# The up product of three more pairs by a scheme of 15 block products, its sums of weights and inputs kept in the gate stage's tiles

## Chip, core and metric

One Trainium2 chip, of which the kernel uses one core. The metric is the device time of one execution in microseconds, as the median of three runs. Inputs and outputs are in fp32.

## What is computed

A gated recurrence (attention) is followed by a low-rank mixer and a two-layer MLP.

```python
# attention, B=4, H=8, S=768, D=48; a is scaled to magnitude <= 0.999 first
for t in range(S):
    S_re, S_im = a_re[t]*S_re - a_im[t]*S_im + outer(k[t], v[t]), a_re[t]*S_im + a_im[t]*S_re
    y[t] = q[t] @ S_re
x = y.transpose(0, 2, 1, 3).reshape(B, S, 384)
# mixer: U is 768x32, V is 32x768, w_ch1 is 384x1536, w_ch2 is 1536x384
u = x + (x.transpose(0, 2, 1) @ U @ V).transpose(0, 2, 1)
out = u + np.maximum(u @ w_ch1, 0) @ w_ch2
```

The change is in `u @ w_ch1`, here called the up product.

## The kernel before

The 4 x 768 tokens are cut into 24 chunks of 128 (`NCH` = 6 chunks to a batch). Most chunks are worked in groups of two. For a group, `gates` (L529) makes the decay factors from a_re and a_im in the tiles x, y, n, z, ar and ai, each of which has one buffer. `prep` (L662) weights and rotates q and k on DVE, transposes them on PE and evicts them with ACT into one of three QK buffers, the ring of L393. `chain` (L691) forms the products within a chunk (`inner`, `corners`), scales QK between them on DVE (`times`, recorded as L329), and carries the state from chunk to chunk (`dk`, `y`).

When the six chunks of a batch are done, three pairs of chunks go through `mixer` (L857), so m runs from 0 to 11: batch 0 gives pairs 0 to 2, batch 3 gives pairs 9 to 11. For each pair the low-rank term is added, u is transposed into uT (L907), the up product fills h, and the down product (`down_two`, L1064, from pair 1 on) adds into the output tile xo. The pairs of one batch run beside the attention of the next batch; only pairs 9 to 11 run alone, at the end.

There are two forms of the up product.

- Plain (`up`, L910), for pairs 0 to 8: 36 matmuls of 128x128 weights with 256 token columns. A group of six fills a PSUM bank, and one ACT Relu of 128x512 evicts it into h.
- `up_fewer` (L922), for pairs from FEWER = 9 on (L227). w_ch1 is seen as 3x3 blocks `a(i, j)` (i is a third of the 1536 outputs, which is four times 128; j is a 128-row block of inputs), and uT as 3x2 blocks `b(j, k)` (k is the chunk of the pair). The plain product is 18 block products. The scheme makes 15 from sums of weight blocks (`combine`, L1006: 13 DVE instructions of 128x512, once) and sums of inputs (L939: 10 DVE instructions for each pair). Each block product is four matmuls of 128x128 with 128 columns, so 60 to a pair. They run in five PSUM accumulations A to E that are not cleared between steps: after every step the running sum is taken out, either copied into a part of h by ACT (L975, six times) or added to it by DVE (L977, recorded as L332, nine times). The next step of the same accumulation has to wait for that. When a part is complete, ACT applies Relu to it (six times). Before the change A and B lie in the PSUM banks tagged Y and C to E in those tagged A, which attention also uses. The combined weights c(0) to c(7) and the input sums x(0) to x(11) lie in the three QK buffers, which are free by then.

The order of all instructions is made in advance by `Plan` (L45): each step is recorded with an engine, a cost, a rank and the buffers it needs; a list scheduler then picks for each engine the ready step of the lowest rank. The ranks of attention steps come from the table URGENCY, and `urgency` (L253) gives the products of the MLP the rank n + 1000 and the small steps around it n - 1000. The engines run exactly this order. While PE has nothing planned before the first MLP product, it issues filler matmuls on the identity (L1222).

Of the kernel before, what the change touches and what calls it, by code (L numbers as in the profile page):

```python
# [23 lines left out]
BLK = 32  # L24

URGENCY = {
    "w1": {0: -424.24, 1: 801.16, 2: -941.63, 3: 764.55, 4: 813.86, 5: -255.72, 6: 1013.64},
    "w2": {0: -182.39, 2: -4.99, 4: 984.13, 6: -117.56, 8: -114.39, 10: -7.53, 12: -119.07},
    "gates": {0: -53.85, 1: -240.4, 2: -197.04, 4: -1081.73, 6: -28.82, 8: -131.88, 10: -81.91, 12: 806.19, 14: -135.86,
        16: -172.78, 18: -1235.03, 20: -1238.39, 22: -793.35},  # L30
    "angles": {0: -716.01, 1: -1088.81, 2: -1448.91, 4: -1014.2, 6: -162.99, 8: 28.61, 10: -297.82, 12: 644.75,
        14: 834.98, 16: 897.12, 18: 629.83, 20: 664.93, 22: -754.36},
    "prep": {0: -721.6, 1: -435.35, 2: -1258.46, 3: -186.16, 4: -178.84, 5: -818.35, 6: -144.43, 7: 728.1, 8: -1457.09,
        9: -198.24, 10: 551, 11: 946.21, 12: -172.65, 13: -5.89, 14: -408.17, 15: -519.54, 16: -1135.98,
        17: -956.56, 18: -1131.69, 19: -157.67, 20: -96.66, 21: 899.53, 22: 814.34, 23: -381.52},
    "levels": {0: 564.72, 1: -778.93, 2: -86.7, 3: -537.84, 4: -1278.59, 5: -136.91, 6: 701.9, 7: 776.18, 8: -1127,
        9: -702.85, 10: -795.56, 11: 2.07, 12: -1232.03, 13: -1063.51, 14: -1125.58, 15: 974.76, 16: 79.03,
        17: -1073.03, 18: 681.53, 19: -464.62, 20: 687.22, 21: -956.1, 22: -13.2, 23: -550.79},
    "rest": {0: -161.27, 1: -1281.74, 2: -47.49, 3: -331.17, 4: -871.19, 5: -748.68, 6: -223.21, 7: -779.64,
        8: -191.99, 9: -545.57, 10: -436.36, 11: -535.13, 12: -1262.49, 13: -76.97, 14: -253.25, 15: -455.92,  # L40
        16: -157.31, 17: -92.4, 18: -977.97, 19: 625.7, 20: -1238.92, 21: -243.55, 22: -90.76, 23: 790.73},
}


# [144 lines left out]
def kernel(  # L189
# [34 lines left out]
    DH = DM // 2  # L224

    PLAIN = 1
    FEWER = B * (S // CH) // 2 - 3  # L227
    NCH = S // CH
    NT = B * NCH
    HH = H // 2  # L230
# [70 lines left out]
    def PE(*a, **kw):  # L301
        plan.add("PE", *a, late=0.17, **kw)
# [87 lines left out]
    AT, DG, VP = [], [], []  # L390
    QKC = singles.tile([128, H, 2, DP], FP, name="QKC")
    nc.gpsimd.memset(QKC, 0.0)
    QKS = [singles.tile([128, 2, H, CH], FP, name="QK%d" % n) for n in range(3)]  # L393
    TS = []
    for n in range(3):
        TS.append(singles.tile([DQ, GC, H * NTOT], FP, name="T%d" % n))
# [45 lines left out]
    def load_a(g):  # L442
        lo, hi = GROUPS[g]
        for nm, src in (("ar", a_re), ("ai", a_im)):
            buffer((nm, g), nm, 1, [128, GC, H, D])
            for i in range(lo, hi):
                SP(c_dma(DM), ("load", (0, 0.5, 3)[g] if g < 3 else lo + 3), lambda nm=nm, src=src, i=i: nc.sync.dma_start(
                    out=get(nm, g)[:, i - lo], in_=rows(src, i)), writes=[(nm, g, i)])
# [80 lines left out]
    def gates(g):  # L529
# [13 lines left out]
            return get(*b)[:, (i - lo) * DM:(i - lo + 1) * DM]  # L543

        def magnitudes():
            for b in (x, y, n):
                buffer(b, "g" + b[0], 1, [128, GC * DM])
            ring(l, "GL", GL)
            ACT(ca, R1, lambda: act(t(x), t(ar), AF.Square), [ar], [x])
            ACT(ca, R1, lambda: act(t(y), t(ai), AF.Square), [ai], [y])  # L550
            DVE(cd, R1, lambda: add(t(x), t(x), t(y)), [y], [x])
            DVE(c_one(W), R1, lambda: nc.vector.tensor_scalar(out=t(x), in0=t(x), scalar1=M2LO, scalar2=M2HI, op0=OP.max,
                                                              op1=OP.min), [], [x])
            ACT(ca, R1, lambda: act(t(n), t(ar), AF.Abs), [ar], [n])
            table(ca, R1, lambda: act(t(l), t(x), AF.Ln), [x], [l])
            table(ca, R1, lambda: act(t(x), t(l), AF.Exp, scale=0.5), [l], [x])
            DVE(cd, R1, lambda: add(t(x), t(x), t(n)), [n], [x])
            table(ca, R1, lambda: act(t(y), t(l), AF.Exp, scale=-0.5, bias=leps), [l], [y])
            table(ca, R1, lambda: act(t(y), t(y), AF.Ln, bias=1.0), [], [y])

            ACT(ca, R1, lambda: act(t(l), t(l), AF.Relu, scale=-0.5, bias=lmax), [], [l])
            DVE(cd, R1, lambda: nc.vector.scalar_tensor_tensor(out=t(l), in0=t(l), scalar=LNMAX, in1=t(y), op0=OP.subtract,
                                                               op1=OP.add), [y], [l])
            table(ca, R1, lambda: act(t(x), t(x), AF.Ln), [], [x])
            table(ca, R1, lambda: act(t(x), t(x), AF.Exp, scale=-1.0), [], [x])
            DVE(cd, R1, lambda: mul(t(x), t(x), t(ai)), [ai], [x])
            ACT(ca, R1, lambda: act(t(n), t(ar), AF.Sign, bias=tiny), [ar], [n])
            for i in range(lo, hi):
                within(i)
# [36 lines left out]
                  [e + (i,)])  # L606

        def turns():
            buffer(z, "gz", 1, [128, GC * DM])

            table(ca, R2, lambda: act(t(x), t(x), AF.Arctan), [], [x])
            DVE(cd, R2, lambda: nc.vector.scalar_tensor_tensor(out=t(z), in0=t(x), scalar=math.pi / 4, in1=t(n),
                                                               op0=OP.subtract, op1=OP.mult), [x, n], [z])
            ACT(ca, R2, lambda: act(t(z), t(z), AF.Identity, scale=1.0 / math.pi, bias=fourth), [], [z])
            for i in range(lo, hi):
                angles(i)
# [45 lines left out]
    def prep(i):  # L662
        R1 = "prep", i
        g = group_of(i)
        qk, QK = ("qk", i), ("QK", i)
        ring(QK, "QK", [a[0:DQ] for a in QKS])
        def weigh():
            a = get(*qk).rearrange("p u h d -> p u (h d)")
            mul(a, a, get("es", i))
# [187 lines left out]
    def mixer(m):  # L857
# [52 lines left out]
        def up(ff):  # L910
# [8 lines left out]
            PE(2.6, RM, products, [uT] + [("w1", f, lo) for f in range(KD)], [ps], takes=[h], steps=4 * KD)  # L919
            ACT(c_act(2 * N), R0, lambda: act(get(*h)[:, ff:ff + 2], get(*ps), AF.Relu), [ps], [h + (ff,)])  # L920

        def up_fewer():  # L922

            if m == FEWER:
                for n in range(3):
                    ring(("wc", n), "QK", [a.rearrange("p u h t -> p (u h t)") for a in QKS])
                combine()
            n3, B0, RU = KF // 3, ("bc", m), ("small", m)  # L930

            def b(j, k):
                return get(*uT)[:, j, k * CH:(k + 1) * CH]

            def x(n, w=1):
                return get("wc", 2)[:, n * CH:(n + w) * CH]

            def put(w, o, a, b, op, reads=(), writes=()):
                DVE(c_dve(w * CH), RU, lambda: nc.vector.tensor_tensor(out=o(), in0=a(), in1=b(), op=op), [uT] + list(reads),  # L939
                    [("wc", 2, n) for n in writes])  # L940

            flat = lambda lo, hi: get(*uT).rearrange("p f t -> p (f t)")[:, lo * CH:hi * CH]
            many = lambda a, w: a.unsqueeze(1).to_broadcast([128, w, CH])
            put(3, lambda: x(0, 3).rearrange("p (w t) -> p w t", t=CH), lambda: flat(0, 3).rearrange("p (w t) -> p w t", t=CH),
                lambda: many(b(1, 1), 3), OP.subtract, (), (0, 1, 2))
            put(1, lambda: x(3), lambda: b(0, 0), lambda: b(1, 0), OP.subtract, (), (3,))
            put(1, lambda: x(4), lambda: x(3), lambda: b(2, 0), OP.add, [("wc", 2, 3)], (4,))
            put(1, lambda: x(5), lambda: x(4), lambda: b(1, 1), OP.add, [("wc", 2, 4)], (5,))
            put(1, lambda: x(6), lambda: b(2, 1), lambda: x(4), OP.subtract, [("wc", 2, 4)], (6,))
            put(2, lambda: x(7, 2).rearrange("p (w t) -> p w t", t=CH), lambda: flat(0, 2).rearrange("p (w t) -> p w t", t=CH),  # L950
                lambda: many(b(2, 1), 2), OP.add, (), (7, 8))
            put(1, lambda: x(9), lambda: b(0, 1), lambda: b(0, 0), OP.subtract, (), (9,))
            put(1, lambda: x(10), lambda: b(0, 0), lambda: b(2, 0), OP.add, (), (10,))
# [6 lines left out]
            def chain(tag, steps):  # L960

                ps = ("few", (m, tag))
                psum(ps, "Y" if tag in "AB" else "A", [128, n3, CH])
                for n, (w, v, to) in enumerate(steps):
                    def products(n=n, w=w, v=v):
                        for q in range(n3):
                            nc.tensor.matmul(out=get(*ps)[:, q], lhsT=w()[:, q * 128:(q + 1) * 128], rhs=v[0](), start=(n == 0 and q == 0),  # L967
                                             stop=True, skip_group_check=True)
                    PE(0.9, RM, products, [uT, ("w1", 0, 0)] + [("wc", 0), ("wc", 1)] + [("wc", 2, k) for k in v[1]], [ps], takes=[h],
                       steps=2 * n3)  # L970
                    i, k = to
                    o = ("part", (m, i, k))
# [12 lines left out]
                return lambda: w1[:, j, i * n3 * 128:(i + 1) * n3 * 128]  # L985

            def c(n):
                return lambda: get("wc", n // 4)[:, n % 4 * n3 * 128:(n % 4 + 1) * n3 * 128]

            def u(j, k):  # L990
                return (lambda: b(j, k)), ()
# [14 lines left out]
        def combine():  # L1006
# [6 lines left out]
            def a(i, j):  # L1013
                return w1[:, j, i * n3:(i + 1) * n3]

            def c(n):
                return get("wc", n // 4)[:, n % 4 * n3:(n % 4 + 1) * n3]

            def put(n, x, y, op, reads=()):
                DVE(c_dve(n3), RC, lambda: nc.vector.tensor_tensor(out=c(n), in0=x(), in1=y(), op=op),  # L1020
                    [("wc", k // 4, k % 4) for k in reads], [("wc", n // 4, n % 4)])
            sub_, add_ = OP.subtract, OP.add
            put(6, lambda: a(2, 0), lambda: a(2, 1), add_)
            put(4, lambda: c(6), lambda: a(0, 1), sub_, (6,))
# [158 lines left out]
                        mixer(m)  # L1183


    waits, later, done = [], [], 0
    for g in range(NG):
        load_a(g)
# [89 lines left out]
```

## Time and profile before

| | us |
|---|---|
| median of three runs | 710.96 (710.59 to 711.04) |
| the profiled execution | 709.66 |
| its span in the trace | 707.9 |
| PE busy | 687.1 (97%) |
| DVE busy | 517.9 (73%) |
| ACT busy | 406.6 (57%) |
| granted PE clock, mean over the span | 0.992 |

Busy times are sums over one engine's instructions; what a change is worth in a stage depends on which engine ends last there. In the trace an fp32 product on PE appears as two records: 324 plain matmuls of the nine plain pairs are the 648 records of L917. The ends of PE records are modelled, so a stall of PE is read from the starts of its instructions and not from gaps in its busy time.

### The profile page before, as it was taken

What the parts mean: (1) busy time and instruction counts of PE and PEld (TensorE: products, weight loads), DVE (VectorE), ACT (ScalarE), POOL (GpSimd) and SP (SyncE); (2) the same over time, 40 slices, a digit from 0 to 9 for tenths busy, and PEclk for the clock granted to TensorE, in tenths of its full rate; (3) what the DMA queues carried; (4) which work ended last, traced back from release to release, by engine and by line L of the source; (5) the groups of instructions that cost most, each with busy time, mean ns of one, the idle gap of its engine ahead of it and who ended that gap; (6) DMA issues with size and microseconds to landing.
All of it is one profiled execution on the core that took longest, in us unless ns stands there. A gap on an engine that the chain in (4) does not pass through costs nothing.

```text
span 707.9 us, 26672 instructions
## 1 busy us (share of the span) xinstructions
PE 687.1 (97%) x12004; PEld 599.7 (85%) x12004; DVE 517.9 (73%) x823; ACT 406.6 (57%) x760; POOL 51.3 (7%) x92
## 2 busy tenths in 40 slices
PE   7989998999999999999999999999999999999998
PEld 6877877877688898888898888888898897999997
DVE  5899998887899787858788578375693665555734
ACT  6796987677797796969695945532413223041230
POOL 5110000011010000001001011000000000000000
PEclk9999998899999999999999999999999999999999
DMA  7876855489423433324134041221201010000000
GB/s 186 180 183 146 179 103 145 92 197 179 103 59 69 87 66 87 72 67 102 20 76 97 5 97 26 52 53 37 48 16 37 3 40 1 12 13 23 6 19 22
DMA packets 165265, 53.22 MB, mean 75 GB/s; under 512 B 154080, under 2 KB 160416, under 8 KB 165152
## 3 DMA queue, kind: packets, MB, share of 16 engines
q1 hardware_dynamic: 161072, 42.26, 27.5%
q0 software_dynamic: 4080, 9.27, 5.6%
q8 instruction: 94, 1.54, 0.9%
q14 instruction: 19, 0.16, 0.1%
HBM read 33.59 MB, written 4.72 MB: 54 GB/s over the span
## 4 chain that ended last, share of the span: by engine, by line
PE 76%; ACT 10%; DVE 7%; issue 3%; DMA 2%; SPq 1%; DVEq 0%; ACTq 0%
PE down L1099 20%; PE up L917 17%; PE few L967 6%; PE inner L717 5%; PE tr L683 5%; PE dk L803 3%; PE y L842 3%; PE down L1056 2%; PE ks ps L788 2%; PE es ps L575 2%; DVE QK L329 2%; ACT x L326 2%; PE y L834 2%; PE ph L633 2%; PE spare L1222 1%
## 5 line engine op out<-in xcount | busy, mean ns | idle before, releaser
L329 DVE TENSOR_TENSOR QK<-QK,T 112x1024 f32<-112x1024 f32 x120 | 145.1, 1217 | 8.1 <-PE corners L767 7.1
L917 PE MATMUL up<-uT,w 128*128 128x256 f32 x648 | 150.2, 383 | 0.0
L917 PEld LDWEIGHTS up<-uT,w 128*128 128x128 f32 x648 | 119.9, 190 | 17.7 <-issue 0.6
L326 ACT ACTIVATE h<-up 128x512 f32<-128x512 f32 x54 | 32.0, 593 | 75.1 <-PE up L917 66.4
L1099 PE MATMUL down<-w,h 128*128 128x192 f32 x396 | 73.5, 330 | 0.0
L686 ACT COPY QK<-tr 112x512 f32<-112x512 f32 x96 | 52.4, 586 | 33.0 <-PE tr L683 32.6
L1099 PEld LDWEIGHTS down<-w,h 128*128 128x128 f32 x396 | 64.0, 190 | 2.9 <-issue 1.3
L1222 PE MATMUL spare<-ident 128*128 128x128 f32 x438 | 62.2, 292 | 1.8 <-POOL ident masks.py:199 1.4
L1222 PEld LDWEIGHTS spare<-ident 128*128 128x128 f32 x438 | 56.0, 201 | 5.7 <-issue 2.0
L717 PEld LDWEIGHTS inner<-QK 112*32 112x32 f32 x4608 | 45.4, 110 | 13.8 <-issue 8.7
L683 PE MATMUL tr<-ident,QKC 128*112 128x128 f32 x384 | 52.8, 275 | 1.5 <-DVE QKC L329 0.9
L717 PE MATMUL inner<-QK 112*32 112x16 f32 (+1 forms) x4608 | 50.7, 190 | 3.3 <-issue 2.9
L329 DVE TENSOR_TENSOR QKC<-qk,cs 128x768 f32<-128x768 f32 x48 | 45.7, 952 | 11.0 <-PE tr L683 6.6
L332 DVE TENSOR_TENSOR xo<-down,xo 128x192 f32<-128x192 f32 (+1 forms) x79 | 29.5, 384 | 29.4 <-PE down L1099 27.5
L683 PEld LDWEIGHTS tr<-ident,QKC 128*112 128x112 f32 x384 | 42.3, 133 | 9.6 <-ACT QK L686 2.5
L1043 POOL DMA_DIRECT2D out_dram<-xo x32 | 18.5, 577 | 332.5 <-DVE xo L332 307.8
L772 ACT COPY AT<-corners 32x128 f32<-32x128 f32 x96 | 24.5, 255 | 31.3 <-PE corners L767 30.3
L975 ACT COPY h<-few 128x512 f32<-128x512 f32 x18 | 10.4, 582 | 51.6 <-PE few L967 51.6
L851 ACT COPY xo<-y 64x192 f32<-64x192 f32 x96 | 30.0, 312 | 11.5 <-PE y L842 10.3
L1099 PE MATMUL down<-stage 128*128 128x192 f32 x198 | 36.6, 328 | 0.0
L723 DVE COPY_PREDICATED DG<-mask,inner 128x128 f32<-128x128 int32 (+1 forms) x72 | 24.3, 340 | 15.7 <-PE inner L717 12.6
L332 DVE TENSOR_TENSOR h<-few,h 128x512 f32<-128x512 f32 x27 | 18.7, 691 | 23.0 <-PE few L967 22.2
(131 smaller groups left out, 1227.3 us busy)
## 6 DMA issues: line engine op xcount, KB each, us to landing
stage<-in_moe_w_ch_dram SPq DMA_DIRECT2D x12, 768.0 KB, 7.5
ar<-in_a_re_dram SPq DMA_DIRECT2D x24, 192.0 KB, 3.4
ai<-in_a_im_dram SPq DMA_DIRECT2D x24, 192.0 KB, 3.7
qk<-in_q_dram SPq DMA_DIRECT2D x24, 192.0 KB, 3.1
qk<-in_k_dram SPq DMA_DIRECT2D x24, 192.0 KB, 4.0
VP<-in_v_dram SPq DMA_DIRECT2D x24, 192.0 KB, 3.8
w<-stage POOLq DMA_DIRECT2D x12, 384.0 KB, 6.0
T<-E SPq DMA_DIRECT2D x44, 96.0 KB, 2.4
```

The source lines that it names most:

```text
L326: return nc.scalar.activation(out=o, in_=i, func=f, **kw)
L329: nc.vector.tensor_tensor(out=o, in0=a, in1=b, op=OP.mult)
L332: nc.vector.tensor_tensor(out=o, in0=a, in1=b, op=OP.add)
L683: nc.tensor.transpose(out=get(*ps)[0:DQ, j], in_=get(*qkc)[:, hh * HH + j].rearrange("p u d -> p (u d)")[:, 0:DQ], identity=ident)
L686: ACT(c_act(HH * CH) - 0.05, R1, lambda u=u, hh=hh, ps=ps: nc.scalar.copy(out=get(*QK)[:, u, hh * HH:(hh + 1) * HH], in_=get(*ps)[0:DQ]), ...
L717: nc.tensor.matmul(out=get(*ps)[js, h], lhsT=k_of(h)[:, js], rhs=part(q_of(h)[:, js], "p"), start=True, stop=True, tile_position=(0, j * BLK))
L772: ACT(0.32, RR, lambda r=r, u=u: nc.scalar.copy(out=get(*ATi).rearrange("p (a u) t -> p a u t", u=2)[r:r + BLK, :, u, BLK:2 * BLK], in_=ge ...
L851: ACT(c_act(HH * D), RR, lambda r=r, u=u: nc.scalar.copy(out=get(*xi).rearrange("p (a u d) -> p a u d", u=2, d=D)[r * HC:(r + 1) * HC, :, ...
L917: nc.tensor.matmul(out=get(*ps)[:, e], lhsT=w1[:, f, (ff + e) * 128:(ff + e + 1) * 128], rhs=get(*uT)[:, f], start=(f == 0), stop=(f == KD ...
L967: nc.tensor.matmul(out=get(*ps)[:, q], lhsT=w()[:, q * 128:(q + 1) * 128], rhs=v[0](), start=(n == 0 and q == 0), stop=True, skip_group_ch ...
L1099: nc.tensor.matmul(out=get(*to)[:, part], lhsT=x(j), rhs=y[:, j], start=(first and j == 0), stop=(j == KH - 1), skip_group_check=not first)
L1222: nc.tensor.matmul(out=spare[0], lhsT=ident, rhs=ident, start=True, stop=True)
```

## The change

The constant FEWER goes from 9 to 6, so pairs 6, 7 and 8 use the scheme as well; pairs 9 to 11 use it before and after. These three pairs run beside the attention of batch 3, which still needs the QK buffers, so the sums move. The six gate tiles become one tile GATE of six areas of 768 columns. When the last gate group is done, the first 512 columns of area n hold c(n) for n up to 5, the other 256 hold x(n) and x(n + 6), and a new tile holds c(6) and c(7). In the ring of each area the scheme's sums come after all the gate groups, so `combine` can only be ordered behind the last of them. QK becomes an ordinary pool of three. For pairs before the last batch the accumulations A and B lie in the PSUM banks tagged M, which up and down products share, and C, D and E in those tagged T, which the transposes share. The URGENCY table is another one throughout, so the order of the attention's instructions changes, by single places before the first MLP product and more widely after it.

```diff
-    "w1": {0: -424.24, 1: 801.16, 2: -941.63, ...
+    "w1": {0: 577.09, 1: -1319.32, 2: 484.43, ...
...
-    FEWER = B * (S // CH) // 2 - 3
+    FEWER = B * (S // CH) // 2 - 6
...
-    QKS = [singles.tile([128, 2, H, CH], FP, name="QK%d" % n) for n in range(3)]
+    GATE = singles.tile([128, 6, GC * DM], FP, name="gate")
+    AREA = {nm: GATE[:, n] for n, nm in enumerate(("x", "y", "n", "z", "ar", "ai"))}
+    AREA.update({nm: AREA[nm].rearrange("p (c h d) -> p c h d", h=H, d=D) for nm in ("ar", "ai")})
+    sums_w = singles.tile([128, 2, KF // 3 * 128], FP, name="sums")
...
-        ring(QK, "QK", [a[0:DQ] for a in QKS])
+        buffer(QK, "QK", 3, [DQ, 2, H, CH])
...
+        def mix_of(n):
+            return GATE[:, n, 0:KF // 3 * 128] if n < 6 else sums_w[:, n - 6]
+
+        def c_of(n):
+            return ("few", n, "w") if n < 6 else ("few", 0, "w%d" % n)
...
-            n3, B0, RU = KF // 3, ("bc", m), ("small", m)
+            n3, RU, late = KF // 3, ("small", m), i0 >= (B - 1) * NCH
...
             def x(n, w=1):
-                return get("wc", 2)[:, n * CH:(n + w) * CH]
+                at = n3 * 128 + n // 6 * CH
+                return GATE[:, n % 6, at:at + CH] if w == 1 else GATE[:, n:n + w, at:at + CH] if n < 6 else GATE[:, n - 6:n - 6 + w, at:at + CH]
...
-                psum(ps, "Y" if tag in "AB" else "A", [128, n3, CH])
+                psum(ps, ("Y" if late else "M") if tag in "AB" else "A" if late else "T", [128, n3, CH])
...
+    for n, nm in enumerate(AREA):
+        for g in range(NG):
+            ring((nm, g), "g" + nm, [AREA[nm]])
+        ring(("few", n), "g" + nm, [GATE[:, n]])
```

More of the change, by code (lines that the diff above doesn't have):

```diff
@@ L26 @@
 URGENCY = {
[L27 to L38, printed above, removed]
@@ L39 @@
-    "rest": {0: -161.27, 1: -1281.74, 2: -47.49, 3: -331.17, 4: -871.19, 5: -748.68, 6: -223.21, 7: -779.64,
-        8: -191.99, 9: -545.57, 10: -436.36, 11: -535.13, 12: -1262.49, 13: -76.97, 14: -253.25, 15: -455.92,
-        16: -157.31, 17: -92.4, 18: -977.97, 19: 625.7, 20: -1238.92, 21: -243.55, 22: -90.76, 23: 790.73},
+    "w1": {0: 577.09, 1: -1319.32, 2: 484.43, 3: -236.69, 4: 471.82, 5: -1058.73, 6: 187.51},
+    "w2": {0: -111.09, 2: 522.21, 4: 896.97, 6: -52.37, 8: 604.14, 10: 640.8, 12: -317.28},
@@ new lines @@
+    "gates": {0: -265.04, 1: 268.17, 2: 43.76, 4: -996.63, 6: 89.37, 8: 509.61, 10: -55.71, 12: 809.99, 14: -95.12,
+        16: 160.61, 18: -122.91, 20: -425.54, 22: -1729.17},
+    "angles": {0: -126.72, 1: -84.17, 2: -1567.87, 4: -1150.68, 6: -325.13, 8: 105.31, 10: 61.73, 12: 732.88,
+        14: -1148.2, 16: 655.25, 18: 538.84, 20: -116.45, 22: 233.15},
+    "prep": {0: -1639.87, 1: -367.99, 2: -1022.47, 3: -12.47, 4: -106.92, 5: -436, 6: -74.87, 7: 260.1, 8: -1682.29,
+        9: 278.7, 10: 47.08, 11: 569.46, 12: -1452.21, 13: -249.3, 14: -287.97, 15: -363.52, 16: -269.7,
+        17: -1664.43, 18: -240.93, 19: 153, 20: -1089.48, 21: -198.95, 22: -127.5, 23: 757.32},
@@ new lines @@
+    "levels": {0: 731.75, 1: -318.03, 2: 17.02, 3: -430.68, 4: -436.08, 5: -170.38, 6: 221.56, 7: 124.72, 8: -1567.59,
+        9: -1453.16, 10: -1698.36, 11: -60.78, 12: 502.58, 13: 523.21, 14: -1475.59, 15: 515.81, 16: -1265.88,
+        17: 487.77, 18: -263.92, 19: 16.81, 20: 723.89, 21: -1759.83, 22: -1111.46, 23: -160.12},
+    "rest": {0: 468.93, 1: -1086.12, 2: 24.25, 3: -218.54, 4: -1119.41, 5: -346.92, 6: 0.68, 7: -1700.8, 8: 681.55,
+        9: -376.72, 10: -229.72, 11: -305.85, 12: -1069.62, 13: 601.71, 14: -282.72, 15: 204.95, 16: 59.77,
+        17: 552.08, 18: -62.45, 19: 466.03, 20: -1105.96, 21: -351.77, 22: -1688.33, 23: 463.92},
@@ L444, in load_a @@
         for nm, src in (("ar", a_re), ("ai", a_im)):
-            buffer((nm, g), nm, 1, [128, GC, H, D])
             for i in range(lo, hi):
@@ L545, in magnitudes @@
         def magnitudes():
-            for b in (x, y, n):
-                buffer(b, "g" + b[0], 1, [128, GC * DM])
             ring(l, "GL", GL)
@@ L608, in turns @@
         def turns():
-            buffer(z, "gz", 1, [128, GC * DM])
             table(ca, R2, lambda: act(t(x), t(x), AF.Arctan), [], [x])
@@ L920, in up @@
             ACT(c_act(2 * N), R0, lambda: act(get(*h)[:, ff:ff + 2], get(*ps), AF.Relu), [ps], [h + (ff,)])
+        def mix_of(n):
+            return GATE[:, n, 0:KF // 3 * 128] if n < 6 else sums_w[:, n - 6]
+        def c_of(n):
+            return ("few", n, "w") if n < 6 else ("few", 0, "w%d" % n)
         def up_fewer():
             if m == FEWER:
-                for n in range(3):
-                    ring(("wc", n), "QK", [a.rearrange("p u h t -> p (u h t)") for a in QKS])
                 combine()
-            n3, B0, RU = KF // 3, ("bc", m), ("small", m)
+            n3, RU, late = KF // 3, ("small", m), i0 >= (B - 1) * NCH
             def b(j, k):
@@ L935, in x, with x_of @@
             def x(n, w=1):
-                return get("wc", 2)[:, n * CH:(n + w) * CH]
+                at = n3 * 128 + n // 6 * CH
+                return GATE[:, n % 6, at:at + CH] if w == 1 else GATE[:, n:n + w, at:at + CH] if n < 6 else GATE[:, n - 6:n - 6 + w, at:at + CH]
+            def x_of(n):
+                return "few", n % 6, "x%d" % (n // 6)
             def put(w, o, a, b, op, reads=(), writes=()):
                 DVE(c_dve(w * CH), RU, lambda: nc.vector.tensor_tensor(out=o(), in0=a(), in1=b(), op=op), [uT] + list(reads),
-                    [("wc", 2, n) for n in writes])
+                    [x_of(n) for n in writes])
             flat = lambda lo, hi: get(*uT).rearrange("p f t -> p (f t)")[:, lo * CH:hi * CH]
             many = lambda a, w: a.unsqueeze(1).to_broadcast([128, w, CH])
-            put(3, lambda: x(0, 3).rearrange("p (w t) -> p w t", t=CH), lambda: flat(0, 3).rearrange("p (w t) -> p w t", t=CH),
+            put(3, lambda: x(0, 3), lambda: flat(0, 3).rearrange("p (w t) -> p w t", t=CH),
                 lambda: many(b(1, 1), 3), OP.subtract, (), (0, 1, 2))
             put(1, lambda: x(3), lambda: b(0, 0), lambda: b(1, 0), OP.subtract, (), (3,))
[L947 to L950, printed above, removed]
+            put(1, lambda: x(4), lambda: x(3), lambda: b(2, 0), OP.add, [x_of(3)], (4,))
+            put(1, lambda: x(5), lambda: x(4), lambda: b(1, 1), OP.add, [x_of(4)], (5,))
+            put(1, lambda: x(6), lambda: b(2, 1), lambda: x(4), OP.subtract, [x_of(4)], (6,))
+            put(2, lambda: x(7, 2), lambda: flat(0, 2).rearrange("p (w t) -> p w t", t=CH),
                 lambda: many(b(2, 1), 2), OP.add, (), (7, 8))
@@ L968, in products @@
                                              stop=True, skip_group_check=True)
-                    PE(0.9, RM, products, [uT, ("w1", 0, 0)] + [("wc", 0), ("wc", 1)] + [("wc", 2, k) for k in v[1]], [ps], takes=[h],
+                    PE(0.9, RM, products, [uT, ("w1", 0, 0)] + [c_of(k) for k in range(8)] + [x_of(k) for k in v[1]], [ps], takes=[h],
                        steps=2 * n3)
@@ L987, in c @@
             def c(n):
-                return lambda: get("wc", n // 4)[:, n % 4 * n3 * 128:(n % 4 + 1) * n3 * 128]
+                return lambda: mix_of(n)
             def u(j, k):
@@ L1014, in a @@
                 return w1[:, j, i * n3:(i + 1) * n3]
-            def c(n):
-                return get("wc", n // 4)[:, n % 4 * n3:(n % 4 + 1) * n3]
+            c = mix_of
             def put(n, x, y, op, reads=()):
                 DVE(c_dve(n3), RC, lambda: nc.vector.tensor_tensor(out=c(n), in0=x(), in1=y(), op=op),
-                    [("wc", k // 4, k % 4) for k in reads], [("wc", n // 4, n % 4)])
+                    [("w1", f) for f in range(KD)] + [c_of(k) for k in reads], [c_of(n)])
             sub_, add_ = OP.subtract, OP.add
```

## Prediction

> **What bounds the kernel now.** I read the slices of the span first, then the groups, the chain that ended last, and the stretches of batch 3.
>
> ```profile
> PE   7989998999999999999999999999999999999998
> DVE  5899998887899787858788578375693665555734
> PEclk9999998899999999999999999999999999999999
> ```
>
> From slice 9 on (about 152 us, where the first up product starts) PE is at 9 in every slice but the last. Before that PE is filled up: the page's group of filler matmuls on the identity is busy for 62.2 us, so the start is bound elsewhere. The change leaves it as it was: 219 fillers are planned before and after, and up to the first MLP products the built programs differ by single places. The granted clock is 1.00 in every later stretch I asked for but the last (0.99), so it is no part of the sum.
>
> ```profile
> L917 PE MATMUL up<-uT,w 128*128 128x256 f32 x648 | 150.2, 383 | 0.0
> L332 DVE TENSOR_TENSOR h<-few,h 128x512 f32<-128x512 f32 x27 | 18.7, 691 | 23.0 <-PE few L967 22.2
> L975 ACT COPY h<-few 128x512 f32<-128x512 f32 x18 | 10.4, 582 | 51.6 <-PE few L967 51.6
> ...
> L326 ACT ACTIVATE h<-h 128x512 f32<-128x512 f32 x18 | 11.3, 630 | 15.2 <-DVE h L332 15.2
> ```
>
> The mean of one PE record (383 ns) is a latency, since records overlap. The rate comes from the chain, where runs of one kind stand with start and length:
>
> ```profile
> 484.24 2.59 PE up L917 x12
> ...
> 648.16 13.55 PE few L967 x120
> ...
> 666.70 10.73 PE down L1099 x66
> ```
>
> So a record of the plain form (256 columns) takes 2.59/12 = 0.216 us, one of the scheme (128 columns) 13.55/120 = 0.113 us, and the 120 come without a gap when PE, DVE and ACT have nothing else to do.
>
> The stretches of batch 3 (PE busy, PEld, DVE, ACT, POOL, with counts) show what lies beside it:
>
> ```profile
> 464.00:484.00 20.00, 20.00 (x429) 17.89 (x418) 18.89 (x30) 2.72 (x5) 1.17 (x2) 1.00 0.13 28
> 484.00:510.00 26.00, 25.93 (x539) 22.48 (x538) 12.72 (x21) 12.37 (x31) 0.54 (x1) 1.00 0.26 54
> 510.00:530.00 20.00, 20.00 (x426) 18.70 (x425) 18.57 (x31) 3.31 (x10) 0.54 (x1) 1.00 0.06 13
> 530.00:556.00 26.00, 26.00 (x491) 22.96 (x490) 11.64 (x19) 9.60 (x23) 1.08 (x2) 1.00 0.12 28
> ```
>
> The rows alternate: around the down products DVE is busy for 94% of the time, around the plain up products for under half. The up phase is where DVE catches up, and that is where the scheme puts its additions. PE bounds batch 3, with DVE close behind.
>
> **What PE saves.** A plain pair is 72 records: 72 x 0.216 = 15.54 us. A pair by the scheme is 13.55 us. That is 1.99 us a pair, 5.97 us for three. Here a rule speaks against the change. The Trainium skill (TensorE: Matmul & The Clock Gate, section Back-to-back issue gap) gives for a stream of weight load and matmul 81 ns at 128 columns and 131 ns at 512, the weight load counting in. An estimate between them is 98 ns at 256, so halving the columns would save only 17%; a pair by the scheme would take 15.54 x (120 x 81)/(72 x 98) = 21.4 us, and three pairs would lose 17.6 us. The rows say that 128 columns cost 0.113/0.216 = 52% of 256, with 0.190 us long weight loads under the matmuls, and this is the same fp32 form in the same kernel. I take the rows.
>
> **What the other engines get.** Per pair DVE has 9 additions x 0.691 = 6.22 us, and 10 input sums, which the trace shows for pairs 9 to 11 at 2.73 us (5.7 + 1.7 + 0.8 for three pairs). That is 8.95 us. ACT's six Relus of 0.593 become six copies of 0.582 and six Relus of 0.630: +3.7 us. In batch 3 ACT is busy 38 us of 136, so this lies beside other work with much room. `combine` (13 x 0.68 = 8.9 us) moves from pair 9, where it lay under a gapless run of 72 down records, to the end of batch 2. There DVE is busy 18.4 us of 34 between 430 and 464: it fits. It can only follow the last gate group, which was finished ahead of the third low-rank product before as well; two of its 13 stand behind the last phase product there. DMA counts are the same and only change places.
>
> **Does DVE then hold PE?** A pair of batch 3 takes 46, 46 and 44 us with DVE busy 31.6, 30.2 and 28.3. After: 40.6 of 44, 39.2 of 44, 37.3 of 42, or 92%, 89%, 89%. On average it fits, so what counts is stretches: from a point where DVE waits for PE to one where PE waits for DVE, DVE's work in the order of the changed program against PE's, both at durations of this trace.
>
> - In the scheme's own part of pair 6 DVE has 13.4 us (9 additions, four scalings of 1.217, small steps) to PE's 18.2. Step by step, each addition is done before the next step of its accumulation: between two steps of A lie two others (1.8 us), the eviction takes 0.9 with its latency, and the scalings stand where `inner`, `corners` or `ks` give more room. Nothing is lost.
> - Before pair 6, from the last phase product to the second block product: DVE 20.8, PE 19.6. PE waits 1.3 us.
> - From the last step of pair 6 to the second `inner` of pair 7's products, which waits for the sixth scaling: DVE 28.9 (six scalings 7.3, four rotations 3.8, ten input sums 2.7, eight steps of the down product's sums 4.4, additions and state the rest), PE 27.0. The first down sum also waits for the last Relu, some 0.7 us in which DVE stands still, partly behind other PE work: with latencies I take 2.5 us.
> - After pair 7, to the first products of the state: DVE 11.5, PE 10.5, so 1.2 us.
>
> That is 5.0 us. The same arithmetic on the program before gives in batch 3 1.7 + 1.0 + 0.5 = 3.2 us; such waits are in its time already. So 1.8 us is new. The scheme's products are also cut by small tiled products in more places (three more changes between full and tiled use of PE; the chain has 12 records in 2.59 us inside a run, and 2.69 start to start before a tiled product): 0.3 us. Batches 1 and 2, reordered, have waits of some 7.7 us by this arithmetic before and 7.8 after: nothing, with 1 us either way. No row shows a scheme's accumulation in banks M and T beside transposes; below, it costs nothing (the steps stand in the order as the banks come free), above, one eviction of 0.7 us for each of the six accumulations on M, 4 us. I take the lower end, because two M banks are held by down products in the same way now.
>
> Sum: -5.97 + 1.8 + 0.3 = -3.9 us. The profiled execution of 709.66 us (span 707.9 and 1.8 around it) becomes 705.8; the median of the runs is 1.3 us above it, so 710.96 - 3.9 = **707.0 us**.
>
> **Rivals.**
> - *The saving arrives whole* (chance 0.27). For: DVE's average of about 90% leaves room, and the waits before did not show in PE's busy time. Against: the stretch of 28.9 to 27.0. It gives 710.96 - 5.97 = 705.0.
> - *DVE becomes the bound of batch 3* (0.18). For: the down phases were at 94% without input sums. The 5.0 us of waits are all new, and M banks cost a little: -5.97 + 5.0 + 0.3 + 0.2 = -0.5, so 710.5; it gives 708.5 to 711.5.
> - *Slower by the eviction chain* (0.05). Place: the 27 additions of pairs 6 to 8, in DVE's queue among scalings. If each finds one scaling of 1.217 us ahead of it, against a room of 0.9 us, 27 x 0.3 = 8.6 us is lost, and six places with one step between lose 0.9 more each, 5.4 us. With the waits above this is about +10 us. From 0.4 of that on (5.3 us) it is measurably slower than before; half of it gives 714. Against: 13.4 us of DVE work in 18.2.
>
> **Numbers.** The likeliest case has 0.50 (705.5 to 708.5). The range of 704.0 to 710.2 takes in most of the whole saving and the better half of the DVE-bound case. What a measurement of this kernel can tell from no change is about 0.2%, 1.4 us: faster means below 709.5. Faster: 0.50 + 0.27 + 0.08 = 0.85; same 0.10; slower 0.05.
>
> **What would show it.** L917 should fall to 432 records and the block products rise to 720, with runs of 0.113 us a record also in batch 3. The time from the third to the fourth low-rank product was 134.3 us (464.4 to 598.7 in the chain). It should shrink by about as much as the total, once products moved across its ends are counted. DVE should be near 90% there, with starts of PE behind scalings and input sums at pair 7. I would be wrong if the block products in batch 3 started further apart than those in the tail, or if batches 1 and 2 moved by more than 1 us.

## The result and the profile after

| | before | after |
|---|---|---|
| median of six runs, us | 710.78 (709.33 to 712.21) | 706.13 (704.18 to 707.35) |
| span of the profiled execution | 707.9 | 702.6 |
| first up product to the start of PE's last matmul | 552.0 | 546.8 |

The ratio of the times is 0.9932, with a 95% interval of 0.9911 to 0.9953: 4.7 us less (3.3 to 6.3). The prediction was 3.9 us less. The third row is read from the starts of PE's instructions in the trace. It is the more exact measure of this change, because the start of the program varies by itself: in all the executions profiled here the first up product started between 150.8 and 155.8 us. I call it the PE stage; it is used for the experiments below. It varies too: in the four traces whose program is the same up to the third low-rank product, the time from the first up product to there is 320.4 to 321.6 us (with the old ranks, in three traces, 311.9 to 312.2). So a difference of 1 us in the PE stage tells nothing with the new order.

The slices of the profile after, PE, DVE and clock:

```profile
PE   7989998999999999999999999999999999999998
DVE  5899998888898887759678487879887787455734
PEclk9999999799999999999999999999999999999999
```

PE is as full as before, and DVE's digits 28 to 34, counted from one (batch 3 after), are now 7 to 9; before they lay between 3 and 9. The groups, in the page's form:

```profile
L916 PE MATMUL up<-uT,w 128*128 128x256 f32 x432 | 98.7, 381 | 0.0
...
L982 ACT COPY h<-few 128x512 f32<-128x512 f32 x36 | 20.8, 584 | 85.2 <-PE few L974 85.1
...
L332 DVE TENSOR_TENSOR h<-few,h 128x512 f32<-128x512 f32 x54 | 37.2, 691 | 30.2 <-PE few L974 26.2
```

L916 (L917 before) has lost the 216 records of three pairs, and additions and copies have doubled at the same duration. The chain of waits shows what a block product takes in batch 3 (start, length, piece), with one run of the tail below:

```profile
487.04 1.22 PE inner L716 x85
488.27 4.66 PE few L974 x40
492.93 0.69 PE corners L766 x50
...
528.67 1.94 PE few L974 x16
...
613.64 13.55 PE few L974 x120
```

40 records in 4.66 us are 0.117 us each, against 0.113 in the tail where nothing else runs: the scheme keeps its pace beside the attention. Here is batch 3 of the kernel after in one stretch (PE, PEld, DVE, ACT, POOL, clock):

```profile
472.60:598.90 126.30, 125.95 (x2685) 118.30 (x2686) 101.03 (x180) 46.63 (x109) 4.36 (x8) 1.00 0.12 28
```

From the third to the fourth low-rank product it took 134.4 us before and takes 126.2 now, a fall that is larger than the whole gain. The counts explain it: 18 down products (0.325 us each) and 16 records of transposes (0.11 us each), 7.6 us in all, are ordered ahead of the third low-rank product after the change. From the third low-rank product to pair 9's first block product, where the same moves count once, it is 154.5 before and 140.8 after: 13.7 us, of which 7.6 are moved and 6.1 are gained. Between the first up product and the third low-rank product the time grew by 8.5 us, so 0.9 us more than was moved there.

### The profile page after: what moved, and what is told of

It is laid out like the page before. It is cut to its first block, busy times and chain, and to the rows that moved or that the text cites. A ratio compares the mean times of both kernels' runs of the same rounds, so it can differ in the third digit from the quotient of the medians.

```text
span 702.6 us, 27047 instructions
## 1 busy us (share of the span) xinstructions
PE 681.1 (97%) x12148; PEld 601.0 (86%) x12148; DVE 540.1 (77%) x877; ACT 418.1 (60%) x778; POOL 51.8 (7%) x92
## 4 chain that ended last, share of the span: by engine, by line
PE 79%; ACT 9%; DVE 7%; issue 3%; DMA 1%; SPq 0%; DVEq 0%; ACTq 0%
PE down L1105 21%; PE few L974 12%; PE up L916 12%; PE inner L716 6%; PE tr L682 5%; ACT gate L326 3%; PE dk L802 3%; PE y L841 3%; PE spare L1232 2%; PE ks ps L787 2%; PE down L1062 2%; PE es ps L575 2%; PE ph L632 2%; PE tot L601 2%; PE y L833 2%
## 5 line engine op out<-in xcount | busy, mean ns | idle before, releaser
L916 PE MATMUL up<-uT,w 128*128 128x256 f32 x432 | 98.7, 381 | 0.0
L916 PEld LDWEIGHTS up<-uT,w 128*128 128x128 f32 x432 | 80.7, 190 | 12.0 <-DVE uT L906 0.2
L326 ACT ACTIVATE gate<-gate 128x768 f32<-128x768 f32 (+1 forms) x91 | 71.0, 792 | 6.2 <-DVE gate L611 2.0
L982 ACT COPY h<-few 128x512 f32<-128x512 f32 x36 | 20.8, 584 | 85.2 <-PE few L974 85.1
L332 DVE TENSOR_TENSOR h<-few,h 128x512 f32<-128x512 f32 x54 | 37.2, 691 | 30.2 <-PE few L974 26.2
L974 PE MATMUL few<-gate,w 128*128 128x128 f32 x336 | 43.1, 277 | 0.0
L974 PEld LDWEIGHTS few<-gate,w 128*128 128x128 f32 x336 | 40.0, 192 | 0.3
```

Of the source, the lines that this page charges most:

```text
L326: return nc.scalar.activation(out=o, in_=i, func=f, **kw)
L332: nc.vector.tensor_tensor(out=o, in0=a, in1=b, op=OP.add)
L916: nc.tensor.matmul(out=get(*ps)[:, e], lhsT=w1[:, f, (ff + e) * 128:(ff + e + 1) * 128], rhs=get(*uT)[:, f], start=(f == 0), stop=(f == KD ...
```

## The experiments

My theory at this point: the gain is PE's columns, and DVE is close enough to PE that waits of about 2 us are new. The rivals: the new order of instructions is what gains, or DVE has slack and nothing new is waited for.

| run | time over the kernel before (95% interval) | PE stage, us |
|---|---|---|
| kernel before | 1 | 552.0 |
| kernel after | 0.9932 (0.9911 to 0.9953) | 546.8 |
| new order, pairs 6 to 8 plain | 1.0058 (1.0035 to 1.0080) | 555.8 |
| old ranks, scheme from pair 6 | 0.9930 (0.9911 to 0.9949) | 547.1 |
| old ranks, scheme from pair 8 | 0.9973 (0.9955 to 0.9990) | 550.5 |
| old ranks, scheme from pair 5 | 1.0134 (1.0082 to 1.0186) | 561.4 |
| input sums twice | 1.0104 (1.0076 to 1.0133) | 559.5 |
| three of the sums twice | 0.9973 (0.9956 to 0.9990) | 550.3 |
| nine of the sums left out | 0.9906 (0.9887 to 0.9925) | 547.7 |
| combine twice | 1.0103 (1.0078 to 1.0129) | 561.9 |
| combine left out | 0.9939 (0.9912 to 0.9965) | 547.4 |
| input sums twice, planned | 1.0025 (1.0006 to 1.0044) | 554.3 |
| combine twice, planned | 1.0011 (0.9989 to 1.0033) | 553.4 |

**Scheme or order?** The first run takes the new tiles and ranks and leaves pairs 6 to 8 in the plain form.

```diff
-    FEWER = B * (S // CH) // 2 - 6
+    FEWER = B * (S // CH) // 2 - 3
```

> The changed kernel with FEWER back at 9: the new tiles and the new table of ranks, but pairs 6 to 8 in the plain form. Theory (the saving is PE's columns, 1.99 us a pair): 5.3 to 6 us above the changed kernel, so about 711 to 712, the time of the kernel before within 1.5 us. Rival (the new order of instructions is what gains): at most 2 us above the changed kernel, about 706 to 708.

It was slower than either side expected: 9.0 us above the kernel after in the PE stage, and 3.8 above the kernel before. So the new order gains nothing by itself. Most of the 3.8 us are two waits of PE in batch 3, each inside a group of `inner`. The profile marks them "issue": it shows nothing that PE waits for. Here is the first (start, length, instruction, and the wait in brackets); the second is 1.46 us long:

```profile
520.86 1.19 PE L716 MATMUL inner<-QK 112*32 112x16 f32 x119
523.59 0.27 PE L716 MATMUL inner<-QK 112*32 112x16 f32 x9 [1.55 <-issue]
```

The last section comes back to waits of this kind. The second run gives the new code the old ranks, that is, it puts the old URGENCY table back.

> The changed kernel with the table of ranks of the kernel before; pairs 6 to 8 by the scheme. Theory: within 2 us of the changed kernel, 705 to 708, since the ranks only have to keep DVE's additions ahead of PE. Rival (the new order is what gains): about the time before, 710 to 711. If the additions need the new order, DVE stalls PE in batch 3 and the time is above 709, with the loss between the third and fourth low-rank product.

It has the time of the kernel after, 547.1 to 546.8 in the PE stage. The new table is worth nothing measurable in the changed kernel; the scheme is what gains. That the new order costs 3.8 us in the plain form was not foreseen by the theory.

**Pair by pair.** With the old ranks, FEWER was set to 8.

> The changed kernel with the old table of ranks and FEWER at 8, so that pair 8 alone of the three uses the scheme. Theory (the gain is PE's columns, pair by pair): from the first up product to the end 1.6 to 2 us less than the kernel before, a third of the gain of all three with that table. Rival (the gain needs the three together, or a place where one wait goes): nothing, or more than 3 us.

1.5 us less than before for one pair; all three with the same ranks give 4.9, or 1.6 a pair. That is just below the theory's 1.6 to 2. PE's columns save 1.99 a pair by the rates, so with all three some 0.4 a pair does not arrive. In that run PE's idle time in batch 3 is 1.5 us, against 0.7 before, and 1.13 of it is one wait marked "issue".

**Does DVE hold PE?** Two runs change the DVE work of the input sums and leave every engine's order alone. For pairs 6 to 8 each sum is issued twice, or nine of ten are left out (the products of those pairs then read old contents of the tiles).

```diff
-DVE(c_dve(w * CH), RU, lambda: nc.vector.tensor_tensor(out=o(), in0=a(), in1=b(), op=op), ...
+DVE(c_dve(w * CH), RU, lambda: [nc.vector.tensor_tensor(out=o(), in0=a(), in1=b(), op=op) for _ in range(1 if late else 2)], ...
```

> The changed kernel with each of the ten input sums of pairs 6 to 8 issued twice in its place: 2.7 us more of DVE a pair, 8.2 us in all, the planned order unchanged. Theory of the prediction (DVE holds PE in the stretch from pair 6 to pair 7 and after pair 7): nearly all of it comes through in those stretches, 4 to 8 us. Rival (PE alone bounds batch 3 and DVE has slack): under 2 us.

> The changed kernel with nine of the ten input sums of pairs 6 to 8 left out (those products then read what lay there), 2.2 us less of DVE a pair. Theory of the prediction: the stretch from pair 6 to pair 7 is bound by DVE, so 1.5 to 4 us less. Rival (no new stall in batch 3): within 1 us of the changed kernel.

By stretches, from the starts of PE's instructions:

| us | after | sums left out | sums twice |
|---|---|---|---|
| third low-rank product to pair 6's block products | 10.67 | 10.67 | 12.04 |
| pair 6's block products | 18.44 | 18.44 | 19.94 |
| to pair 7's | 26.76 | 26.51 | 31.97 |
| pair 7's | 18.61 | 18.61 | 18.41 |
| to pair 8's | 25.17 | 25.16 | 29.96 |

Without the sums PE gains 0.25 us in one stretch and nothing elsewhere, and in the stretch of batch 3 shown above PE is idle for 0.35 us of 126.3. So DVE does not hold PE in the kernel after, and the theory of the prediction falls at this point. (The median of that run lies 0.26% below the kernel after, with intervals that overlap; its PE stage does not.)

But with the sums twice, 12.7 us are lost in batch 3. First, more was added than the 8.2 us of the expectation. DVE's timeline in that run has pairs of equal sums:

```profile
483.24 0.61 DVE L946 TENSOR_TENSOR gate<-gate,uT 128x128 f32<-128x128 f32 x2
483.76 0.61 DVE L946 TENSOR_TENSOR gate<-uT 128x128 f32<-128x128 f32 x2
```

The second sum of a pair writes again what the first has just written, and it starts 0.03 us after the first ends. A pair takes 0.52 us from start to start, where one sum takes 0.20 in the kernel after. From start to start the copies add 10.0 us. Second, the granted clock falls. This is PE's timeline in that run (start, length, instruction), and below it the stretches around it, whose last three columns are granted clock, DMA share and GB/s:

```profile
513.51 1.14 PE L1105 MATMUL down<-stage,h 128*128 128x192 f32 x6
517.21 1.11 PE L682 MATMUL tr<-ident,QKC 128*112 128x128 f32 x8 [2.56 <-DVE QKC L329]
518.25 1.11 PE L833 MATMUL y<-VP,AT 64*64 64x48 f32 x32
```

```profile
514.00:518.00 4.00, 1.44 (x12) 1.18 (x11) 3.83 (x12) 0.14 (x1) 0.00 (x0) 1.00 0.00 0
518.00:524.00 6.00, 6.00 (x200) 5.52 (x199) 2.84 (x6) 2.20 (x6) 0.00 (x0) 0.51 0.54 104
524.00:530.00 6.00, 6.00 (x71) 5.75 (x71) 5.67 (x11) 2.25 (x4) 0.54 (x1) 0.92 0.05 16
```

PE waits 2.56 us for a rotation that stands behind the doubled sums, while DVE is busy for 3.83 of 4 us. After the wait the granted clock is 0.51. The 32 records of `y` take 1.04 us from start to start (518.25 to the next group at 519.29), against 0.61 in the kernel after. A second wait, of 2.92 us before pair 8, is followed by half clock for another 3.4 us. So PE pays for these two waits twice: 5.5 us of waiting, and 4.0 us of slower records in the two stretches at half clock. With the smaller waits before and in pair 6, 7.7 of the 12.7 us are waits.

A third run doubles only the last three sums. From start to start that adds 3.0 us in all.

> The changed kernel with only the last three of the ten input sums of pairs 6 to 8 issued twice, some 0.6 to 0.8 us more of DVE a pair, 2 us in all. If DVE's slack in batch 3 is nil: about 2 us more, at each of the three pairs, and no drop of the granted clock since no single wait of PE is long. If there is slack of about a microsecond a pair: nothing. If stalls multiply what is added, as with all ten twice: 3 us or more.

Batch 3 takes 128.9 us, 2.6 more, with waits near each pair and no drop of the clock; one of the waits, 0.96 us, is marked "issue". So most of what is added to DVE here comes through at once, and what is taken away gains nothing.

**The sums of weights.** Each instruction of `combine` is issued twice or not at all (for `range(2)` and `range(0)` in the same manner as above; then some or all of the combined weights come out different, and without it the new tile is zeroed at the start).

> The changed kernel with each of the 13 instructions of combine issued twice in its place at the end of batch 2 (some of the combined weights come out different from it, the work on PE is the same): 8 to 9 us more of DVE there, once. The prediction's claim (combine fits beside PE's work, DVE has room between 430 and 464): under 2 us more, and the time from the first up product to the first block product grows by under 2 us. Rival (DVE has no slack at that place either): 5 to 9 us more, before the first block product.

> The changed kernel with the 13 instructions of combine left out (the scheme's products read what lies in the tiles; the new tile for two of the sums is zeroed at the start), 8.9 us less of DVE at the end of batch 2. The prediction's claim (combine fits beside PE's work): the time from the second to the third low-rank product falls by under 1 us. Rival (part of it is on the path already): 2 to 6 us less.

Left out, the time from the second to the third low-rank product is 162.4 us, against 162.3 in the kernel after: the claim of the prediction holds, `combine` is covered in full. Twice, that stretch takes 177.0, 14.7 more. Of these, 2.2 arise between 370 and 378 us, long before `combine`: a wait marked "issue" of 1.57 us (1.03 in the kernel after), and 3.4 us at half clock behind it. The other 12.2 lie where `combine` is, for some 9.4 us of added work from start to start, again with waits (here y waits for the state on DVE) and the clock after them, 0.54 from 466 to 476:

```profile
459.15 1.15 PE L1105 MATMUL down<-w,h 128*128 128x192 f32 x6
465.03 0.45 PE L833 MATMUL y<-VP,AT 64*64 64x48 f32 x4 [4.73 <-DVE GM L332]
467.76 1.09 PE L833 MATMUL y<-VP,AT 64*64 64x48 f32 x28 [2.28 <-DVE G L332]
```

**Capacity, or an order fitted to its costs?** Both doubled runs again, with the doubled cost told to the planner.

```diff
-DVE(c_dve(w * CH), RU, lambda: [
+DVE((1 if late else 2) * c_dve(w * CH), RU, lambda: [
```

> As with all ten input sums of pairs 6 to 8 issued twice, but the planner is told the doubled cost of these steps, so that it makes the order for it. If DVE lacks capacity in batch 3 (rival): the time from the first up product to the end stays within 3 us of the run with all ten twice, that is 10 us or more above the changed kernel. If the order was only fitted to the costs it was given (theory): at most 5 us above the changed kernel, and no drop of the granted clock in batch 3.

> As with combine issued twice (again some combined weights come out different), but the planner is told the doubled cost. Theory (the order is fitted to the given costs): at most 5 us above the changed kernel from the first up product to the end, in place of 15. Rival (DVE lacks capacity at the end of batch 2): 10 us or more.

Neither side was right. For the sums the PE stage is 7.5 us above the kernel after in place of 12.7, for `combine` 6.6 in place of 15.1 (some 12, without what arose long before `combine`). A new order wins back 5.2 and some 6 us: that part was the fitted order. In the run of the sums one long wait remained:

```profile
530.34 1.24 PE L716 MATMUL inner<-QK 112*32 112x16 f32 x127
533.78 0.24 PE L716 MATMUL inner<-QK 112*32 112x16 f32 x1 [2.20 <-issue]
```

It is marked "issue", and the clock was at a half for 3.4 us around its end. By an estimate from these two figures it cost some 4 us (2.2, and half of 3.4), so about 3.5 of the 7.5 would be left for DVE. In the other run no wait of PE in batch 3 is longer than 1.41 us and the clock did not drop. What is left may be DVE's lack of capacity or the table of ranks, which was not searched anew; these runs do not separate them.

**Further back.** With the old ranks, FEWER was set to 5, so that pair 5 uses the scheme too.

> The changed kernel with the old table of ranks and FEWER at 5: pair 5 by the scheme as well. PE saves 2 us more in columns, but pair 5's products now have to wait for the last gate group, and the attention of batch 2 that comes before it loses six groups of plain products as cover. Theory (the place of the sums sets how far back the scheme can go): slower than the changed kernel by 2 to 10 us, with waits of PE in batch 2 before the third low-rank product. Rival (PE's columns are all that counts): 1.5 to 2 us faster than the changed kernel.

14.3 us above the same ranks with three pairs. Pair 5's block products cannot start before the last gate group and `combine` behind it are done: `combine` ends at 457.8 us, they start at 458.0. From 429 us on until then the attention of batch 2 has no product of the MLP beside it. The stretches around it:

```profile
424.00:436.00 12.00, 8.72 (x315) 7.49 (x313) 9.39 (x14) 6.82 (x11) 1.12 (x2) 1.00 0.09 29
436.00:447.00 11.00, 6.82 (x144) 5.44 (x145) 10.48 (x16) 4.33 (x13) 0.81 (x1) 0.53 0.15 26
447.00:461.00 14.00, 12.16 (x336) 10.54 (x334) 12.45 (x23) 9.90 (x21) 0.76 (x1) 1.00 0.42 88
```

PE is busy for 8.7 of 12 us and 6.8 of 11, and runs at half clock for 10 us after the waits. With the sums kept in the gate tiles, and with these ranks, pair 6 is the first pair for which the scheme pays. No version that does the whole work and beats the kernel after came out of the runs.

## Why the prediction was right

**The saving on PE, 5.97 us: right.** From start to start, the plain products of pairs 6 to 8 took 48.9 us of PE before; the block products take 42.5 in the kernel after and 42.8 with the old ranks. That is 6.1 to 6.4 us saved, under either order. From the third low-rank product to the tail the gain is 6.1 us once moved work is counted. The row was the better guide than the sustained rates that the prediction set against it: 0.117 us a record in batch 3, 0.113 in the tail, and no 17.6 us of loss.

**combine at no cost: right,** and shown by leaving it out.

**The chain of evictions: right.** In batch 3 the block products run at their pace; the rival that ends slower did not occur.

**New waits on DVE, 1.8 us: wrong.** They are at most 0.25. The 3.2 us that the same arithmetic gave for the kernel before are not in its trace either: PE is idle in batch 3 for 0.7 us before and 0.35 after. The mis-sized term is DVE's 28.9 us against PE's 27.0 in the stretch from pair 6 to pair 7. I added the durations of DVE's rows. They sum to 29.3 us in the trace of after, as predicted, but DVE is occupied for only 25.7 of the 28.6 us that the stretch lasts. Most instructions that follow another directly start before that one ends, on average by 0.09 us (42 of 48 times in this stretch). PE's side was too small as well: PE takes the 28.6 us with 0.2 us of idle time, where I had 27.0. No run shows what the missing 1.6 us are. With 25.7 us of work in 28.6 it is DVE that waits. DVE's timeline shows the overlap (start, length):

```profile
508.12 1.09 DVE L946 TENSOR_TENSOR gate<-uT 128x384 f32<-128x384 f32 x3
509.12 0.29 DVE L946 TENSOR_TENSOR gate<-gate,uT 128x128 f32<-128x128 f32 x1
509.32 0.29 DVE L946 TENSOR_TENSOR gate<-uT 128x128 f32<-128x128 f32 x1
509.52 0.29 DVE L946 TENSOR_TENSOR gate<-gate,uT 128x128 f32<-128x128 f32 x1
```

Each sum of 0.29 us starts 0.20 after the one before it, so a sum of this size costs DVE a third less than its row says. I counted the overlap of PE's records and not that of DVE's.

"DVE at 92%, 89%, 89%" was too high as well, but mostly for another reason. It stands for 117.0 us, 90.1 of the three windows and 26.9 added; batch 3 shows 101.0 us of 126.3, which is 80%. Of the 16.0 us between them, 8.0 are `combine`: it was in those windows before and leaves them with the change, and I did not take it out. The overlap of additions and sums is 2.4. The rest is work that is now ordered ahead of the third low-rank product.

**Full and tiled use, 0.3 us: not contradicted.** The block products' own changes are in the 42.5 us above. PE's other work from the third low-rank product to the tail takes 0.5 us more than before, moved work counted once; whether changes between full and tiled use make it was not traced. With 6.3 us saved and 0.3 us less idle time, this makes the 6.1.

**Batches 1 and 2, 0 with 1 us either way: at the edge.** The trace of after shows 0.9 us lost ahead of the third low-rank product. Three other traces with the same program up to there show 0.9 to 2.1. A wait of PE stands out that the kernel before does not have:

```profile
367.48 1.26 PE L716 MATMUL inner<-QK 112*32 112x16 f32 x121
369.77 0.25 PE L716 MATMUL inner<-QK 112*32 112x16 f32 x7 [1.03 <-issue]
```

It is 0.64 to 1.58 us long in those traces. It comes with the new order: with the old ranks that part takes 312.0 us against 311.9 before, but batch 3 then gives 5.0 us and not 6.1, with a wait of the same kind there.

So the sum was -6.1 in batch 3 and +0.9 ahead of it, -5.2 in the PE stage, where I had -3.9. That -3.9 came so near is in part luck. The 1.8 us of waits on DVE did not come, and about half of their size was lost at a place that I had put at nothing, in good part to a wait that I had not thought of. Of the cases, the measurement lies nearer to the likeliest one in the median and nearer to "the saving arrives whole" in the PE stage; the mechanism was that of the second. What I had not seen at all is how little room the order leaves: DVE stands at 80% and PE does not wait, and still most of what is added to DVE in the two places tried reaches the end.

## What to carry to other kernels

Cost a block product by the rate of its own row at its own width, and queued work on DVE by its start-to-start times: sums of durations overstate a run of short instructions, here by a seventh (29.3 to 25.7). An order made in advance for given costs can keep an engine at 80% off the path and still leave it little slack, so leave work out to see whether it is on the path, add some to see how far it is from it, and expect two different answers. Before a buffer gets a second use behind its first, ask what work would stand without cover while it waits for the first to end.

## What the hardware showed beside this

**The clock.** After a wait of 2.56 us PE's granted clock was at a half for 6.8 us, after one of 2.92 us for 3.4, and after the row of waits up to 4.7 us in the run with `combine` twice for 10.2. The length of a single wait does not settle it: in that same run one of 1.57 us was followed by 3.4 us at half clock, while one of 1.58 in the run without the sums, and those of 1.55 and 1.46 with the new order alone, were followed by none.

**Waits without an engine.** Behind the first up product the 13 traces have 25 waits of PE over 0.3 us that are marked "issue", 17 of them before a product of `inner`, up to 2.20 us long. Each ends 1.2 to 1.7 us after a 16 KB packet of the queue that the page calls "q8 instruction" has landed; of PE's starts without a wait only 7% lie so behind one. So PE most likely waits for its own instructions to be loaded. No run changed the loading, so this is not shown by experiment. In every order these waits fall elsewhere: 0.67 and 0.61 us in the kernel before, 1.03 in the kernel after, 1.03, 1.55 and 1.46 with the new order and plain pairs. An order can win or lose by them what it wins or loses on DVE.
